# A retention layer with a swish MLP on one Trainium2 core: attention insertions merged, and loads, casts and transposes of the last batches moved

## The chip, the core and the metric

The kernel runs on one core of a Trainium2 chip. The metric is device microseconds of one execution. Times of the kernel before are 294.99 us in the median of three runs (294.67 to 295.45).

The engines are named as in the profile: PE is TensorE (matmuls; PEld its weight loads), DVE is VectorE, ACT is ScalarE, POOL is GpSimd, SP is SyncE. SPq stands for SP's queue of transfers: every load, store and DMA transpose here but one is issued by SP, in program order.

## The reference: what is computed

Eight batches (B = 8) of eight heads (H = 8), 576 rows (S) and a head size of 64 (D). Attention without softmax, with a decay per head:

```python
scores = scale * np.matmul(q, k.transpose(0, 1, 3, 2))
gamma = 1.0 - 2.0 ** (-5.0 - np.arange(H, dtype=np.float32))
Dmat = np.where(rel >= 0, gamma[:, None, None] ** rel[None, :, :], 0.0)
ret = scores * Dmat[None, :, :, :]
return np.matmul(ret, v).astype(np.float32)
```

Its result, as x of 4608 rows by 512, goes through an MLP: h = x @ w_in (512 to 2048), g = h * sigmoid(beta * h), out = g @ w_out (2048 to 512).

## The kernel before, in words

**Blocks of the MLP.** The rows are cut into nine blocks of 512: of each batch the first 512 rows (MB), and as block 8 the last 64 rows of all eight batches together, the tail. Blocks are worked in the order 0 to 6, 8, 7. A block is an up phase and a down phase. `up` (L717) makes one of 16 columns of the hidden layer: four matmuls of 512 columns into a PSUM bank `ph` (L724), then an activation on ACT into `gT` (L726). `down` (L750) makes a quarter of one of four row groups `ms`: four matmuls into the bank `po` (L759), and after the last quarter a copy to `ot` (L766) and a store.

**Attention in insertions.** The attention of batch u must be done before block u's up phase reads `xT`. It is cut in pieces that are inserted between the MLP's matmuls as runs of small 64x64 matmuls:
- `d_sc` (L478, matmuls L489): scores of eight chunks of 64 rows. Its first half (x = 0) uses the first pair of transposed keys `kT` of the batch, its second half (x = 1) the second pair; each half is 32 matmuls into two PSUM banks `sc`. `masks` (L496) multiplies them on DVE by a triangle into `R`.
- `d_st` (L500, matmuls L507): the products of keys and values of four chunks, 32 matmuls; its `chain` (L515, L519) adds them to running states on DVE and copies the states to `sbd` on ACT.
- `d_out` (L522): the products of `R` and values (L538, 64 matmuls), then of queries and states (`cross`, L551, 56 matmuls in two parts). The second part waits for a small DVE memset, the fence (L542). `evict` (L566) copies four banks `O` to `xT`, on DVE and ACT by turns.

`scores(u)` (L954) is one insertion: d_st(u, 1) and both halves of d_sc(u), in this order on PE. `outputs(u)` (L961) is d_out(u) with d_st(u + 1, 0). `early_states(2)` (L951) is d_st(2, 0) alone. The tail counts as u = 8.

**Data of a batch.** `load_q` (L84) brings q in two transfers of 512 KB, `load_kv` (L96) a quarter of k and one of v, 256 KB each. On POOL `pre_q` (L294) scales q, `pre` casts k (L323) and scales v (L301). `x_q` and `x_k` (L331) are DMA transposes of q and k, two each for a batch: x_k(b, 0) makes the first pair of `kT`, x_k(b, 1) the second. The program gives the transfers eight DMA semaphores in turn, so that each waits for the eighth before it.

**What sets the order.** The scheduler is off; the order of each engine is the order in which the code is recorded. `fill` is a list of 16 up steps and 16 down steps of a block; a step is four full matmuls. `base[n]` is the place of the n-th block's first step, written b4, b5, b6 for blocks 4 to 6. `streams` are lists of pairs (place in fill, step), and `merged` (L779) records all of them by place, each just ahead of the fill step of that number. `pair_prep` (L970) gives the places at which the data of a pair of chunks are loaded, cast and transposed, counted back from `at`. So a place decides what stands ahead of what on SP, POOL, DVE, ACT and PE alike.

PSUM has eight banks in four groups by tag: mm 3, O 2, sc 2, st 1. The `ph` and `po` of the MLP use mm.

Of the kernel before, what the change touches and what calls it, by code (L numbers as in the profile page):

```python
# [19 lines left out]
def kernel(  # L20
# [88 lines left out]
    tail_tiles, tail_q = {}, []  # L109
# [168 lines left out]

    def pre_q(b, n):

        if n == 0:
            batch[b] = dict(qs=sb.tile([P, CB, H, D], BF16, name="qs", tag="qs", bufs=2),
                            qT=sb.tile([P, CB, HP, P], BF16, name="qT", tag="qT", bufs=2))
# [12 lines left out]

    def pre(i, js=(0, 1)):

        b, c = seq[i]
        if 0 not in js:  # L300
            nc.gpsimd.tensor_tensor(live[i]["vn"], kv_tiles.pop(i)[:, 1], gains(gv, c), ALU.mult)  # L301
            return
        if c % 2 == 0:
            vns[b, c // 2] = sb.tile([P, 2, H, D], BF16, name="vn", tag="vn", bufs=VB)
        vn = vns[b, c // 2][:, c % 2]
        if b is None:
            tq, tk, tv = tail_tiles.pop(c)
            qk = sb.tile([P, 2, H, D], BF16, name="kn", tag="kn", bufs=4)
            qkT = sb.tile([P, 2, HP, P], BF16, name="kT", tag="kT", bufs=4)
            for to, hs in turned:  # L310
                nc.gpsimd.tensor_tensor(qk[:, 0, to], tq[:, hs], gains(gq, CB)[:, hs], ALU.mult)  # L311
                nc.gpsimd.tensor_copy(qk[:, 1, to], tk[:, hs])
            nc.gpsimd.tensor_tensor(vn, tv, gains(gv, CB), ALU.mult)
# [7 lines left out]
        live[i] = dict(kn=kn[:, c % 2], kT=kT[:, c % 2], vn=vn)  # L321
# [11 lines left out]
    def x_q(b, u):  # L333
        turn(batch[b]["qT"][:, 2 * u:2 * u + 2], batch[b]["qs"][:, 2 * u:2 * u + 2])
# [17 lines left out]
    def half(x):  # L352
        return slice(x * D, (x + 1) * D)
# [123 lines left out]

    def d_sc(u, xs=(0, 1)):  # L478

        R = {x: sb.tile([P, 2, 2, HP, TL], BF16, name="R", tag="R", bufs=4) for x in xs}  # L480
        sc = {}
        for x in xs:
            for j in range(2):
                sc[x, j] = psum.tile([P, 2, HP, TL], F32, name="sc", tag="O" if x and u > 1 else "sc", bufs=2)
            for cl in range(2):
                for p in range(HP):
                    for j, hh in spread:
                        c = 4 * x + 2 * cl + hh
                        nc.tensor.matmul(columns(u, sc[x, j][half(hh), cl, p, :]), piece(u, c)["kT"][half(j), p, half(hh)],  # L489
                                         q_of(u, c, j, p), start=cl == 0 and p == 0, stop=True, skip_group_check=True)  # L490
        mask = tri[1 if u == B else 0][:].unsqueeze(1).to_broadcast([P, 2 * HP, TL])
        batch.setdefault(u, {})["R"] = R

        def masks(x):
            for j in range(2):
                nc.vector.tensor_tensor(R[x][:, j].rearrange("k c p q -> k (c p) q"),  # L496
                                        sc[x, j].rearrange("k c p q -> k (c p) q"), mask, ALU.mult)
        return masks

    def d_st(u, x):  # L500

        S = [psum.tile([P, 2, HP, D], F32, name="st", tag=t, bufs=n) for t, n in (("st", 1), ("O", 2) if u == 1 else ("mm", 3))]
# [19 lines left out]
    def d_out(u):  # L522
# [10 lines left out]
        if u >= B - 1:  # L533
            own = [(cc, pp + 2 * y, hh, hh if other else 1 - hh)
                   for other in range(2) for cc in range(CB) for pp in range(2) for y in range(2) for hh in range(2)]
        for n, (cc, p, hh, j) in enumerate(own):
            h = head_of(u, p, j)
            last = nc.tensor.matmul(to(2 * cc + hh, p, h % 2), piece(u, 2 * cc)["vn"][half(hh), h, :],  # L538
                                    columns(u, R[cc // 2][half(hh), j, cc % 2, p, :]),
                                    start=cc == p % 2 == 0, stop=False, skip_group_check=True)  # L540
            if n + 1 == (len(own) if u < B - 1 else len(own) // 2):
                fence = nc.vector.memset(fenced[:], 0.0)  # L542
                after(fence, last)

        def cross(flip):
            for n, (cc, pp, y, j) in enumerate((cc, pp, y, j) for cc in range(CB) for pp in range(2) for y in range(2) for j in range(2)):
# [6 lines left out]
                if flip and n < 2:  # L553
                    after(m, fence)

        cross(0)

        def evict():
            for n, ((hh, y), o) in enumerate(O.items()):
# [6 lines left out]
                (nc.scalar.copy if n % 2 else nc.vector.tensor_copy)(x, o)  # L566
        return lambda: cross(1), evict
# [176 lines left out]
    pos_, ots, held = {}, {}, []  # L744

# [4 lines left out]
    def down(m, ms, f0, fn=4, n0=0, nn=d_model):  # L750

        gT = gts[m]
        if f0 == 0:
            pos_[ms] = psum.tile([P, d_model], F32, name="po", tag="mm" if m or ms < 3 else "st", bufs=3 if m or ms < 3 else 1)
# [11 lines left out]
        (nc.scalar.copy if m == 0 else nc.vector.tensor_copy)(ot, po[:, :nn])  # L766
# [184 lines left out]
    def early_states(u):  # L951
        d_st(u, 0)()

# [14 lines left out]
    lo6 = base[B - 2] + 3  # L968

    def pair_prep(i, at):  # L970
        b, c = seq[i]
        if b is None:
            early, late = ((-23, -12, -7), (-18.5, -8, -6.5)) if c == 0 else ((-11, -3, 7.5), (-6, 1, 8))
            return [(lo6 + x, f) for j, at3 in enumerate((early, late))
                    for x, f in zip(at3, (F(load_tail, c + j), F(pre, i + j), F(x_tail, i + j)))]
# [6 lines left out]
        if c == 0:  # L982
            if b == XB + 1:
                st += [(at - 30.1, F(load_kv, n)), (at - 30, F(x_k, XB, 1)), (at - 30, F(load_kv, n + 1))]
            sooner = 4 if b == B - 1 else 0
            st += [(at - 30 - sooner, F(load_q, b, (u,))) for u in range(2)] + [(at - 20 - sooner + x, F(pre_q, b, x)) for x in range(4)]
            st += [(at - (18 if b > B - 3 else 14) + 1.5 * x, F(x_q, b, x)) for x in range(2)]
        early = b == XB + 1 and c > 0
        loads = [] if b == XB + 1 and c == 0 else [(at - 29.7 + x / 10, F(load_kv, n + x)) for x in range(2)] if early else \
            [(at - 28 + 2 * x - (7 if b == B - 1 and c else 5 if b == B - 1 else 4 if b == B - 2 and c else 0), F(load_kv, n + x)) for x in range(2)]  # L990
        soon, turn_k = (24 if c else 20, 19 if c else 15.5) if b == B - 1 else (22, 11.5) if b == XB + 1 and c == 0 else (16, 13 if c else 11.5)
        return st + loads + [(at - soon, F(pre, i)), (at + 1 - soon, F(pre, i + 1)), (at - turn_k, F(x_k, b, c // 2))]

    streams.append([(base[1] + 17, F(early_states, XB))])
    for n in range(1, B - 1):
        lo, hi = (base[n] + 17, base[n + 1] - 9.5) if n == 1 else (base[n] + 3, base[n + 1] - 14)
        at = (lo, hi)
        work = [(n + 1, hi - 0.5, hi + 6)] if n == 1 else [(n + 1, hi - 1, hi + 6.5)]
        if n == B - 2:
            at = (lo, lo + 7, lo + 14, lo + 18)  # L1000
            work = [(B - 1, lo + 7, lo + 12.5), (B, lo + 20.5, lo + 25.5)]
        for x, t in enumerate(at):
            streams.append(pair_prep((n + 1) * CB + 2 * x, t))
        for u, t, t2 in work:
            streams.append([(t, F(scores, u)), (t2, F(outputs, u))])
# [31 lines left out]
```

## Time and profile before

| what | number |
|---|---|
| median of three runs | 294.99 us |
| the profiled execution's own time | 294.8 us |
| its span in the profile | 293.1 us |
| granted PE clock | 1.00 |
| busy: PE, PEld | 284.2 us, 147.0 us |
| busy: DVE, ACT, POOL | 104.2 us, 145.9 us, 109.9 us |
| bytes moved by DMA | 53.99 MB, mean 184 GB/s |
| median from issue to landing: q, k, v load | 5.9, 5.9, 5.3 us |
| the same: transpose of k, of q; store | 4.6, 3.6; 3.6 us |

A row of the groups or of the timeline names the line in the code, the engine, the operation, what is written and read, and how many there are. In a timeline the first column is the start from the beginning of the span and the second the length, both in us; a bracket at the end gives idle time of that engine just before, and what ended it. The chain of work that ended last is followed back from the last instruction, at each step to what released it. Records of a few matmuls are missing from the trace. Blocks 2 to 5 take about 30.2 us each: block 4's up phase starts at 141.8 us, its down phase at 155.5 us, block 5 at 172.2 us.

### The profile page before, as it was taken

The numbers are of one execution on the slowest core, as the hardware profiler recorded it, in microseconds if no ns is written. First come the engines' busy times: TensorE is split into PE (matmuls) and PEld (weight loads), VectorE is DVE, ScalarE is ACT, GpSimd is POOL, SyncE is SP. The second block draws the span as 40 slices with busy tenths as digits, with TensorE's granted clock in tenths as the row PEclk, the third lists the DMA queues.
The fourth block names the chain that finished last, engine by engine and source line by source line (L and its number), as shares of the span: only waits on it lengthen the run. The fifth ranks groups of instructions, "written<-read, shape, count | busy, mean of one in ns | idle before, by whom it ended". The sixth has DMA issues, their size and how long they took to land.

```text
span 293.1 us, 7933 instructions
## 1 busy us (share of the span) xinstructions
PE 284.2 (97%) x3373; PEld 147.0 (50%) x3404; DVE 104.2 (36%) x223; ACT 145.9 (50%) x262; POOL 109.9 (37%) x219
## 2 busy tenths in 40 slices
PE   7899999999999999999999999999999999999995
PEld 2554456885544554455445544554554544444443
DVE  5874566606620650065104520354053500110012
ACT  5566537882387335743473348334870168007600
POOL 3866037954640834371329407763422000000000
PEclk9999999999999999999999999999999999999999
DMA  7999999999999999949999939989896210131011
GB/s 222 304 366 386 378 279 266 188 179 242 231 139 268 282 192 242 235 74 163 234 241 210 197 105 273 187 177 228 200 176 106 73 39 0 36 72 38 0 72 72
DMA packets 121986, 53.99 MB, mean 184 GB/s; under 512 B 97744, under 2 KB 114400, under 8 KB 121952
## 3 DMA queue, kind: packets, MB, share of 16 engines
q1 hardware_dynamic: 121920, 53.49, 82.4%
q8 instruction: 26, 0.43, 0.7%
q14 instruction: 8, 0.07, 0.1%
q10 hardware_dynamic: 32, 0.01, 0.0%
HBM read 36.71 MB, written 9.44 MB: 157 GB/s over the span
## 4 chain that ended last, share of the span: by engine, by line
PE 94%; DMA 2%; issue 1%; POOL 1%; SPq 1%; DVE 0%; POOLq 0%
PE po L759 42%; PE ph L724 38%; PE ph L739 4%; DMA kvn<-in_k_dram 2%; PE sc L489 2%; PE O L538 2%; PE st L507 2%; PE O L551 1%; POOL kn L373 1%; PE st L448 1%; PE O L417 0%; SPq L104 0%; POOL vn L373 0%; PE ph L892 0%; SPq L84 0%
## 5 line engine op out<-in xcount | busy, mean ns | idle before, releaser
L759 PE MATMUL po<-w_out_sb,gT 128*128 128x512 bf16 (+2 forms) x573 | 125.1, 373 | 2.4 <-issue 2.1
L726 ACT ACTIVATE gT<-ph,beta_sb 128x512 bf16<-128x512 f32 (+1 forms) x144 | 91.3, 643 | 48.0 <-PE ph L724 47.6
L724 PE MATMUL ph<-xT,w_in_sb 128*128 128x512 bf16 (+1 forms) x567 | 113.3, 357 | 0.5
L759 PEld LDWEIGHTS <-gT 128*128 128x128 bf16 x593 | 56.1, 98 | 63.8
L724 PEld LDWEIGHTS <-w_in_sb 128*128 128x128 bf16 x576 | 56.0, 98 | 55.2 <-DVE first L515 0.5
L766 DVE COPY ot<-po 128x512 f32<-128x512 f32 (+2 forms) x33 | 22.2, 672 | 72.3 <-PE po L759 69.6
L496 DVE TENSOR_TENSOR R<-sc,tri 128x512 bf16<-128x512 f32 x30 | 18.7, 682 | 61.5 <-PE sc L489 61.5
L294 POOL TENSOR_TENSOR qs<-qn,gq 128x256 bf16<-128x256 f32 (+1 forms) x36 | 26.5, 764 | 37.3 <-DMA qn<-in_q_dram 36.0
L323 POOL CAST kn<-kvn 128x128 bf16<-128x128 f32 (+1 forms) x78 | 22.7, 331 | 30.7 <-DMA kvn<-in_k_dram 30.6
L301 POOL TENSOR_TENSOR vn<-kvn,gv 128x512 bf16<-128x512 f32 x26 | 27.1, 1045 | 4.9 <-DMA kvn<-in_v_dram 4.4
L566 ACT CAST xT<-O 128x512 bf16<-128x512 f32 x14 | 7.5, 589 | 31.8 <-PE O L551 31.8
L519 ACT CAST sbd<-warm 128x256 bf16<-128x256 f32 x18 | 7.3, 405 | 25.7 <-DVE warm L515 20.7
L739 PE MATMUL ph<-xT,w_in_sb 128*128 128x512 bf16 x54 | 12.5, 379 | 0.1
L515 DVE TENSOR_TENSOR warm<-st,first 128x256 f32<-128x256 f32 x20 | 8.4, 421 | 9.6 <-PE st L507 8.4
L515 DVE TENSOR_TENSOR first<-st,warm 128x256 f32<-128x256 f32 x25 | 10.6, 425 | 2.5
L566 DVE CAST xT<-O 128x512 bf16<-128x512 f32 x14 | 9.0, 686 | 5.7 <-PE O L551 5.7
L742 ACT ACTIVATE gT<-ph,beta_sb 128x512 bf16<-128x512 f32 x14 | 8.6, 687 | 4.5 <-PE ph L739 4.4
L311 POOL TENSOR_TENSOR kn<-tln,gq 128x128 bf16<-128x128 f32 (+1 forms) x12 | 5.7, 472 | 13.1 <-DMA tln<-in_q_dram 8.3
L212 POOL CAST w_in_sb<-wt 128x256 bf16<-128x256 f32 (+1 forms) x15 | 7.8, 538 | 4.7 <-DMA wt<-in_moe_w_in_dram 4.7
L519 ACT CAST sbd<-first 128x256 bf16<-128x256 f32 x18 | 7.3, 405 | 2.3 <-DVE first L515 0.3
L739 PEld LDWEIGHTS <-w_in_sb 128*128 128x128 bf16 x56 | 5.2, 98 | 6.1 <-issue 0.3
L229 DVE TENSOR_SCALAR w_out_sb<-wt,rbeta_sb 128x512 bf16<-128x512 f32 x13 | 5.9, 484 | 5.1 <-DMA wt<-in_moe_w_out_dram 5.1
(133 smaller groups left out, 164.6 us busy)
## 6 DMA issues: line engine op xcount, KB each, us to landing
qn<-in_q_dram SPq DMA_DIRECT2D x16, 512.0 KB, 5.9
kvn<-in_k_dram SPq DMA_DIRECT2D x32, 256.0 KB, 5.9
kvn<-in_v_dram SPq DMA_DIRECT2D x32, 256.0 KB, 5.3
out_dram<-ot SPq DMA_DIRECT2D x31, 256.0 KB, 3.6
wt<-in_moe_w_out_dram SPq DMA_DIRECT2D x8, 512.0 KB, 9.4
wt<-in_moe_w_in_dram SPq DMA_DIRECT2D x5, 512.0 KB, 9.5
wt<-in_moe_w_in_dram SPq DMA_DIRECT2D x6, 256.0 KB, 5.7
tln<-in_q_dram SPq DMA_DIRECT2D x8, 128.0 KB, 4.4
```

The source lines that it names most:

```text
L294: nc.gpsimd.tensor_tensor(batch[b]["qs"][:, cs, to], q_tiles[b][:, hs, cs].rearrange("p h i d -> p i h d"), gq[:, cs, hs].unsqueeze(3).to_ ...
L301: nc.gpsimd.tensor_tensor(live[i]["vn"], kv_tiles.pop(i)[:, 1], gains(gv, c), ALU.mult)
L323: nc.gpsimd.tensor_copy(kn[:, c % 2, to], t[:, 0, hs])
L496: nc.vector.tensor_tensor(R[x][:, j].rearrange("k c p q -> k (c p) q"), sc[x, j].rearrange("k c p q -> k (c p) q"), mask, ALU.mult)
L515: nc.vector.tensor_tensor(new[:], add, sums[(c - 1) % 2][:], ALU.add)
L519: e((sbq[c] if c < NC - 1 else ends[u])[:], new[:])
L566: (nc.scalar.copy if n % 2 else nc.vector.tensor_copy)(x, o)
L724: nc.tensor.matmul(ph, w_in_sb[:, ko, fo * P:(fo + 1) * P], xts[m][:, ko, :, w], start=(ko == 0), stop=(ko == KO - 1))
L726: nc.scalar.activation(gts[m][:, fo, :, w], ph, ACT.Silu, scale=beta_sb[:, fo:fo + 1])
L739: nc.tensor.matmul(phs[f][:], w_in_sb[:, ko, f * P:(f + 1) * P], xts[m][:, ko], start=(ko == 0), stop=(ko == KO - 1))
L759: nc.tensor.matmul(po[:, x:y], gT[:, fo, ms, :], w_out_sb[:, fo, n0 + x:n0 + y], start=(fo == 0), stop=(fo == FO - 1), skip_group_check=m < 2)
L766: (nc.scalar.copy if m == 0 else nc.vector.tensor_copy)(ot, po[:, :nn])
```

## The change

- Batch 2: early_states is gone; `scores_with_states(2, 2)` does its two state products between the two halves of its scores, two steps ahead of where scores(2) was (base[2] - 12 instead of base[2] - 10). The copy of the first row group's `po` of block 1 goes to ACT (`on_scalar`).
- Batches 3, 4 and 5: scores at the same places, outputs of 3 and 4 too.
- Batch 6: its scores are made together with the outputs of batch 5, in one insertion `outputs_with_scores(5, 6)` at b5 - 4 (outputs(5) was at b5 - 7.5, scores(6) at b6 - 15). Their banks are mm, mm and mm, st. The copy of block 4's third row group goes to ACT, and all four copies of the outputs to `xT` too.
- Batch 7: its scores are made together with both state products of batch 6, `scores_with_states(7, 6)`, at b5 + 16, the border of block 5's up and down phases. outputs(6) stays at about b6 - 8, and `last_scores` (second state product of batch 7, scores of the tail) is at b6 + 16, outputs(7) at b6 + 22, the tail's outputs at b6 + 28.5 as before.
- The data of batches 6 and 7 are placed by a new `whole_prep`, which for each batch first places loads of q and k and v, then casts of k, transposes, and scaling of v. The tail's loads, casts and transposes get new places too.
- Batch 2's second key transpose is recorded ahead of batch 3's first k load instead of behind it.
- The tail's scaled q and cast k use the tiles of the tag `qs` instead of `kn`; `qT` and `vn` tiles are taken later.

The core of the diff:

```diff
@@ -475,31 +484,35 @@
+    BANKS = dict(mm=3, O=2, sc=2, st=1)
+
+    def d_half(u, x, tags):
+
+        R = batch.setdefault(u, {}).setdefault("R", {})
+        R[x] = sb.tile([P, 2, 2, HP, TL], BF16, name="R", tag="R", bufs=4)
+        sc = [psum.tile([P, 2, HP, TL], F32, name="sc", tag=t, bufs=BANKS[t]) for t in tags]
...
-    def d_st(u, x):
+    def d_st(u, x, tags=None):
...
@@ -965,14 +982,32 @@
+    def scores_with_states(u, s):
+        first = d_half(u, 0, ("mm", "mm"))
+        first()
+        chains = [d_st(s, 0, ("O", "O")), d_st(s, 1, ("sc", "sc"))]
+        d_half(u, 1, ("mm", "st"))()
+        for f in chains:
+            f()
+
+    def outputs_with_scores(u, v):
+        first = d_half(v, 0, ("mm", "mm"))
+        first((0,))
+        cross, evict = d_out(u, plain=True)
+        first((1,))
+        second = d_half(v, 1, ("mm", "st"))
+        cross()
+        evict(es=(nc.scalar.copy,) * 2)
+        second()
+
+    def last_scores():
+        chain, masks = d_st(B - 1, 1), d_sc(B)
+        chain()
+        for x in range(2):
+            masks(x)
...
@@ -981,28 +1016,39 @@
-                st += [(at - 30.1, F(load_kv, n)), (at - 30, F(x_k, XB, 1)), (at - 30, F(load_kv, n + 1))]
...
+                st += [(at - 30.1, F(x_k, XB, 1)), (at - 30, F(load_kv, n)), (at - 30, F(load_kv, n + 1))]
...
+    def whole_prep(b, q_in, kv_in, q_pre, k_pre, q_turn, k_turn, v_pre):
+        i, st = b * CB, [(q_in + u / 2, F(load_q, b, (u,))) for u in range(2)] + [(q_pre + x, F(pre_q, b, x)) for x in (0, 2)]
+        st += [(q_turn + 1.5 * u, F(x_q, b, u)) for u in range(2)] + [(k_turn + 1.5 * u, F(x_k, b, u)) for u in range(2)]
+        for x in range(CB):
+            st += [(kv_in + x, F(load_kv, full.index(i + x))), (k_pre + x, F(pre, i + x, (0,))), (v_pre + x, F(pre, i + x, (1,)))]
+        return st
...
-    streams.append([(base[1] + 17, F(early_states, XB))])
-    for n in range(1, B - 1):
+    for n in range(1, B - 3):
...
+        if n == 1:
+            on_scalar.add((1, 0))
+            streams.append([(base[2] - 12, F(scores_with_states, XB, XB)), (hi + 6, F(outputs, XB))])
+        else:
+            streams.append([(hi - 1, F(scores, n + 1))] + ([(hi + 6.5, F(outputs, n + 1))] if n < B - 4 else []))
+    b4, b5, b6 = base[B - 4], base[B - 3], base[B - 2]
+    streams.append(whole_prep(B - 2, b4 - 2, b4, b4 + 6, b4 + 10, b4 + 12, b4 + 15.5, b4 + 14))
+    streams.append(whole_prep(B - 1, b4 + 18, b4 + 19, b4 + 20, b4 + 24, b5 - 3, b4 + 27, b5 - 3))
...
+    on_scalar.add((B - 4, 2))
+    streams.append([(b5 - 4, F(outputs_with_scores, B - 3, B - 2)), (b5 + 16, F(scores_with_states, B - 1, B - 2)),
+                    (b6 - 8, F(outputs, B - 2)), (b6 + 16, F(last_scores)), (b6 + 22, F(outputs, B - 1)), (b6 + 28.5, F(outputs, B))])
```

The pair of batch 5's last chunks is still placed by `pair_prep`: its k and v loads at b4 - 10 and b4 - 8, its casts at b4 + 2 and b4 + 3, and its transpose x_k(5, 1) at b4 + 5, as before. scores(5) is recorded at b4 + 17.

More of the change, by code (lines that the diff above doesn't have):

```diff
@@ L107 @@
     span_tiles = {}
-    tail_tiles, tail_q = {}, []
+    tail_tiles, tail_q, tail_qk = {}, [], {}
     def load_tail(t):
@@ L476, in after @@
         tc.add_manual_dep(later.ins, earlier.ins.name, mybir.DependencyInfo(mybir.DependencyClass.Sync, mybir.DependencyReason.DATA))
-    def d_sc(u, xs=(0, 1)):
[L480 to L498, printed above, removed]
@@ L500, in d_st, with masks @@
-    def d_st(u, x):
-        S = [psum.tile([P, 2, HP, D], F32, name="st", tag=t, bufs=n) for t, n in (("st", 1), ("O", 2) if u == 1 else ("mm", 3))]
+    BANKS = dict(mm=3, O=2, sc=2, st=1)
[3 more added lines that the diff above has]
+        sc = [psum.tile([P, 2, HP, TL], F32, name="sc", tag=t, bufs=BANKS[t]) for t in tags]
+        for cl in range(2):
+            for p in range(HP):
+                for j, hh in spread:
+                    c = 4 * x + 2 * cl + hh
+                    nc.tensor.matmul(columns(u, sc[j][half(hh), cl, p, :]), piece(u, c)["kT"][half(j), p, half(hh)],
+                                     q_of(u, c, j, p), start=cl == 0 and p == 0, stop=True, skip_group_check=True)
+        mask = tri[1 if u == B else 0][:].unsqueeze(1).to_broadcast([P, 2 * HP, TL])
+        def masks(js=(0, 1)):
+            for j in js:
+                nc.vector.tensor_tensor(R[x][:, j].rearrange("k c p q -> k (c p) q"),
+                                        sc[j].rearrange("k c p q -> k (c p) q"), mask, ALU.mult)
+        return masks
@@ L503, in d_st @@
+    def d_sc(u, xs=(0, 1)):
+        parts = {x: d_half(u, x, ("O", "O") if x and u > 1 else ("sc", "sc")) for x in xs}
+        return lambda x: parts[x]()
+    def d_st(u, x, tags=None):
+        S = [psum.tile([P, 2, HP, D], F32, name="st", tag=t, bufs=n) for t, n in [(t, BANKS[t]) for t in tags or ("st", "O" if u == 1 else "mm")]]
         for cl in range(2):
@@ L532, in d_out, with products, cross @@
         own = [(cc, p, hh, j) for cc in range(CB) for p in range(HP) for hh, j in spread]
-        if u >= B - 1:
+        if u >= B - 1 and not plain:
             own = [(cc, pp + 2 * y, hh, hh if other else 1 - hh)
                    for other in range(2) for cc in range(CB) for pp in range(2) for y in range(2) for hh in range(2)]
[L536 to L546, printed above, removed]
+        def products(own, at):
+            for n, (cc, p, hh, j) in enumerate(own):
+                h = head_of(u, p, j)
+                last = nc.tensor.matmul(to(2 * cc + hh, p, h % 2), piece(u, 2 * cc)["vn"][half(hh), h, :],
+                                        columns(u, R[cc // 2][half(hh), j, cc % 2, p, :]),
+                                        start=cc == p % 2 == 0, stop=False, skip_group_check=True)
+                if n + 1 == at:
+                    fence = nc.vector.memset(fenced[:], 0.0)
+                    after(fence, last)
+            return fence
+        def cross(flip, fence=None):
+            n = 0
+            for cc, pp, y, j in [(cc, pp, y, j) for cc in range(CB) for pp in range(2) for y in range(2) for j in range(2)]:
                 c, p = 2 * cc + (j ^ flip), pp + 2 * y
@@ L565, in evict @@
                     o = o.rearrange("k p i c s -> k (p i) c s")
-                (nc.scalar.copy if n % 2 else nc.vector.tensor_copy)(x, o)
-        return lambda: cross(1), evict
+                es[n % 2](x, o)
+        fence = products(own, len(own) if u < B - 1 or plain else len(own) // 2)
+        cross(0)
+        return lambda: cross(1, fence), evict
     def o_pre(j, a, e=nc.gpsimd):
@@ L744 @@
     pos_, ots, held = {}, {}, []
+    on_scalar = set()
     def release(n):
@@ L991, in pair_prep @@
-        soon, turn_k = (24 if c else 20, 19 if c else 15.5) if b == B - 1 else (22, 11.5) if b == XB + 1 and c == 0 else (16, 13 if c else 11.5)
+            [(at - 28 + 2 * x, F(load_kv, n + x)) for x in range(2)]
+        soon, turn_k = (22, 11.5) if b == XB + 1 and c == 0 else (16, 13 if c else 11.5)
         return st + loads + [(at - soon, F(pre, i)), (at + 1 - soon, F(pre, i + 1)), (at - turn_k, F(x_k, b, c // 2))]
-    streams.append([(base[1] + 17, F(early_states, XB))])
-    for n in range(1, B - 1):
-        lo, hi = (base[n] + 17, base[n + 1] - 9.5) if n == 1 else (base[n] + 3, base[n + 1] - 14)
[L997 to L1002, printed above, removed]
-            streams.append(pair_prep((n + 1) * CB + 2 * x, t))
-        for u, t, t2 in work:
-            streams.append([(t, F(scores, u)), (t2, F(outputs, u))])
+    def whole_prep(b, q_in, kv_in, q_pre, k_pre, q_turn, k_turn, v_pre):
[4 more added lines that the diff above has]
+        return st
```

49 lines of the change are left out of this document (26 added, 23 removed).

## The prediction

> **What bounds the kernel now.** I read the page's busy times first, then its chain of work that ended last, then that chain in order of time.
>
> ```profile
> PE 284.2 (97%) x3373; PEld 147.0 (50%) x3404; DVE 104.2 (36%) x223; ACT 145.9 (50%) x262; POOL 109.9 (37%) x219
> PE 94%; DMA 2%; issue 1%; POOL 1%; SPq 1%; DVE 0%; POOLq 0%
> ```
>
> TensorE (PE) is the bound; no other engine passes 50%. After 25 us PE runs full matmuls of 512 columns, one each 0.216 us, with **insertions** of small 64x64 attention matmuls between them. So the change can win only what insertions cost, and lose only where PE must wait. An insertion, from PE's timeline (start, length, line):
>
> ```profile
> 95.00 1.03 PE L759 MATMUL po<-w_out_sb,gT 128*128 128x512 bf16 x4
> 95.96 0.45 PE L507 MATMUL st<-vn,kn 64*64 64x64 bf16 x32
> 96.23 0.76 PE L489 MATMUL sc<-qT,kT 64*64 64x64 bf16 x64
> 97.14 6.85 PE L759 MATMUL po<-w_out_sb,gT 128*128 128x512 bf16 x31 [0.16 <-issue]
> ```
>
> The fourth full matmul starts at 95.00 + 3 x 0.216 = 95.65, the next recorded one at 97.14; less one slot of 0.216 that is 1.28 us. But 31 full matmuls are recorded up to the next insertion where the program has 32: the first record after the insertion is missing, so the insertion takes 1.28 - 0.22 = 1.06 us for 96 small matmuls. In the same way early_states at 65 us takes 0.47 us for 32 and outputs at 104 us 1.55 us for 152. The slopes are 0.59/64 = 9.2 ns and 0.49/56 = 8.7 ns a matmul, so about 0.2 us is **fixed per insertion**.
>
> The next view is SP's timeline around the start of block 4 (141.8 us), because SP issues every load, store and DMA transpose in program order.
>
> ```profile
> 142.00 1.68 SPq L772 DMA_DIRECT2D out_dram<-ot  x2
> 145.79 1.23 SPq L331 DMA_TRANSPOSE kT<-kn  x1
> 147.08 1.16 SPq L84 DMA_DIRECT2D qn<-in_q_dram  x2
> 148.28 0.51 SPq L96 DMA_DIRECT2D kvn<-in_k_dram  x1
> 148.83 2.32 SPq L96 DMA_DIRECT2D kvn<-in_v_dram  x1
> 151.20 2.57 SPq L96 DMA_DIRECT2D kvn<-in_k_dram  x1
> 153.81 1.00 SPq L96 DMA_DIRECT2D kvn<-in_v_dram  x1
> ```
>
> The transpose at 145.79 is x_k(5, 1), the second half of batch 5's keys. It waits for POOL's casts, is issued ahead of batch 6's loads, and lands at 149.0. Its reader is the second half of scores(5):
>
> ```profile
> 156.43 0.45 PE L507 MATMUL st<-vn,kn 64*64 64x64 bf16 x32
> 156.71 0.87 PE L489 MATMUL sc<-qT,kT 64*64 64x64 bf16 x64
> 157.73 0.38 PE L759 MATMUL po<-w_out_sb,gT 128*128 128x512 bf16 x1 [0.16 <-issue]
> ```
>
> The second 32 of the 64 sc begin 32 x 9 ns after 156.71, at 157.0. So the keys have 8 us to spare now.
>
> **The change, part by part.**
>
> 1. *Fewer insertions.* Small and full matmuls stay the same in number (1680 small ones from early_states on); insertions go from 15 to 13: early_states joins scores(2), scores(6) joins outputs(5), and scores(7) with states 6 takes the place of two. Two times 0.2 = **-0.4 us**. In the last blocks PE also waits 0.09 us for a ScalarE activation at 214.5 us, behind the state copies of scores(7) (matmul starts 306 ns apart instead of 216); that insertion moves to the border of the up and down phases, where no activation follows the copies: -0.1. Three gaps of 0.1 us inside insertions (157.0, 195.7, 218.1 us), with no wait at those instructions, may stay or go: 0 to -0.3, taken as -0.1. Sum **-0.6 us**.
>
> 2. *New readers and banks, covered.* Batch 2's insertion starts at 67.8 us instead of 70.0. Its second key half is now transposed right behind the first (issued 61.8, landed 66.2), so it lands about 67.5; it is read after sc 32 + st 64, at 67.8 + 96 x 9 ns = 68.7. Cover 1.2 us; without it PE waits the shortfall. The bank for that half is emptied by ScalarE (on_scalar, about 0.64 us from 67.9, done 68.6): 0 to 0.1 lost. The first down after it needs the first mask (VectorE 0.68 us from 68.3): 69.0 against 69.1. The eight state adds end near 75, outputs(2) starts at 77. At outputs(5) with scores(6) the fence sits behind one mask, which ends 1.3 us into the insertion, while cross(1) comes at 1.5. ScalarE's four xT evictions (0.59 each) take 2.4 us against 16 x 0.216 = 3.5 us of downs before their reader. At scores(7) the banks come free as activations 13 to 15 end, each within 0.1 us of need. All at 0, at most +0.3 together.
>
> 3. *Data sooner: what the keys of batch 5 meet.* In the new SP order whole_prep puts batch 6's two q loads (b4 - 2) and eight k and v loads (b4 to b4 + 3) **ahead of x_k(5, 1)** (b4 + 5), which keeps its place. Its keys are ready as before (145.8), but the program uses eight DMA semaphores in turn, so each transfer waits for the eighth before it, and transfers land in order: all 87 issued from 37 to 160 us landed in the order of issue. Landing by landing: batch 5's last v lands at 145.9 now, 145.7 then; store 0.6 (142.0 to 146.5 to 147.2: 0.65 apart); two q loads 1.65 + 1.6 (1.6 apart at 95, 123, 154 us; 2.8 once); store 0.6; eight k and v loads at 1.1 (0.92 to 1.2 where several follow each other, at times 2.2); the transpose 0.9 behind loads. That is 145.7 + 0.6 + 3.25 + 0.6 + 8.8 + 0.9 = **159.85**. SP issues it when the eighth before it, batch 6's first k, has landed (about 151.3), so issue is not what is last. PE wants it at 157.0 - 0.2 (part 1, batch 2's share) = 156.8. PE waits **3.0 us** in the middle of scores(5). The ends: all at their fastest (0.55, 3.1, 0.55, 8 x 0.92, 0.85) gives 158.1, a wait of 1.3; at their slowest (0.65, 4.5, 0.65, 8 x 1.2, 1.4) 162.5, a wait of 5.7. I take 3.0, from the rows met most often. Nothing can hide it: PE takes its matmuls in order, so all that stands behind these 32 waits too, and nobody's work becomes shorter.
>
> 4. *What follows.* The four transposes of batch 6 come directly behind and land by about 164; they are read at outputs(5), near 169.7 with the wait in. Batch 7's loads land to about 177, its transposes by about 183; scores(7) comes near 188.6. POOL's tail products wait for outputs(6) (near 197) and need some 11 us (per tail piece 3 products of 0.47, 3 casts of 0.35, 1.04); their last transpose lands near 212, last_scores is at 219. Cover of 5 us or more each: 0.
>
> **Sum**: -0.6 + 3.0 = +2.4 us on the profiled run's 294.8 us (span 293.1 and 1.7 around it), so 297.2. That run lies 0.2 under the median 294.99, so the forecast for a median is **297.3 us**.
>
> **Rivals.**
>
> *A, the forecast*: the key transpose is held behind batch 6's loads, PE waits 1.3 to 5.7 us. For it: the SP order is in the program, and no transfer overtook another. Chance 0.77.
>
> *B, the transpose does not stand behind the loads' data.* Mechanism: it is issued at about 151.3 and lands 3.2 to 4.6 us later, as the 145.79 one (3.2) and the 61.85 one (4.3) did, whatever is still in flight. It decides if it lands by 156.8. Then only part 1 is left: 294.8 - 0.6 + 0.2 = 294.4, not slower. Against it: the transpose at 87.9 us, with four stores ahead, took 4.9 us and landed last. Chance 0.13 (with a small remainder of a wait under 1.3 us).
> The Trainium skill, page "DMA: Bandwidth & Descriptors", section "Queues, rings and completion order", says that completion is not first in, first out for an issuing engine, since a DMA that uses fewer rings may finish earlier. The trace's 87 landings in order do not show that.
>
> *C, the wait also costs clock.* PE would idle longer than anywhere in this trace after its first matmul (0.35 us at most, at 9.9 us), and the granted clock is 1.00 throughout, so no row shows what an idle PE loses. Bounds: nothing, or half speed for as long as it stood idle, 3.0 us of work done at half rate, +1.5: 298.8. Chance 0.06.
> The Trainium skill, page "TensorE: Matmul & The Clock Gate", section "Why this matters for your kernels", wants no gap over about 3 us, one idle window setting the clock to half. By its window of 3.4 us C would add an estimated 1.7 us; a free-running window is not surely filled by 3 us.
>
> *D, a second late arrival* (batch 6's keys at outputs(5), batch 7's at scores(7)): needs transfers 5 us slower than worked out; 1 to 3 us more, 299.3. Chance 0.04. That the change does not do what it says is part of A: data comes sooner for batch 6 and later for batch 5.
>
> **Chances.** Over 0.3% (0.9 us, about what a measurement of this kernel can tell) slower: A but for waits under 1.5 us, C, D: 0.82. Within: most of B and those short waits: 0.14. Faster: B with all small gains: 0.04. Range 295.6 to 299.6 leaves out B and the worst of A, C and D.
>
> **What would show it.** Right: in scores(5) PE's sc group (32 + 32) is split by an idle time of about 3 us that a DMA kT ends, near 157 to 160 us; SP's line shows the kT transpose after eight kvn loads; every other insertion reads 0.2 us + 9 ns a matmul; later blocks are shifted by a constant. Wrong: no idle time there (B), granted clock under 1.00 after it (C), or PE waiting at outputs(5) or scores(7) (D).

## The result: slower, with one long wait and a lowered clock

| what | before | changed |
|---|---|---|
| median | 295.22 us (six runs, 294.67 to 295.57) | 299.5 us (six runs, 297.97 to 300.58) |
| ratio | | 1.0143, 95% interval 1.0121 to 1.0165 |
| the profiled execution: time, span | 294.8 us, 293.1 us | 300.51 us, 298.8 us |

The change makes the kernel 4.3 us slower in the median; the sum of the prediction was +2.4 us, 297.3 us for a median. First the changed kernel's page: busy times, the shares of the chain that ended last, and the group of the scores' matmuls.

```profile
PE 285.8 (96%) x3375; PEld 147.5 (49%) x3404; DVE 101.5 (34%) x219; ACT 148.4 (50%) x266; POOL 109.2 (37%) x219
...
PE 87%; SPq 5%; DMA 4%; issue 1%; POOL 1%; DVE 0%; POOLq 0%
...
L498 PE MATMUL sc<-qT,kT 64*64 64x64 bf16 x416 | 5.7, 195 | 3.9 <-DMA kT<-kn 3.9
```

PE's share of the chain falls from 94% to 87%, and SP's queue and DMA have 9% where they had 3%: for a stretch the end hangs on transfers. The scores' row names the transfer, the key transpose. PE's timeline of the changed kernel shows the place, the second half of scores(5):

```profile
156.70 0.45 PE L520 MATMUL st<-vn,kn 64*64 64x64 bf16 x32
156.98 0.44 PE L498 MATMUL sc<-qT,kT 64*64 64x64 bf16 x32
161.26 0.45 PE L498 MATMUL sc<-qT,kT 64*64 64x64 bf16 x32 [3.85 <-DMA kT<-kn]
161.90 1.91 PE L779 MATMUL po<-w_out_sb,gT 128*128 128x512 bf16 x4 [0.19 <-issue]
```

The 64 scores that stood together before are split by 3.85 us of idle time. And the four full matmuls behind them take 1.91 us, where four took 1.03 before. The table by stretches of the changed kernel says why; its columns are the stretch, its length, the busy time and number of instructions of five engines, the granted clock, the DMA share and GB/s.

```profile
155.00:157.00 2.00, 2.00 (x45) 0.89 (x46) 0.00 (x0) 1.37 (x2) 0.88 (x3) 1.00 0.96 214
157.00:161.00 4.00, 0.41 (x52) 0.30 (x37) 1.29 (x2) 0.00 (x0) 2.56 (x7) 1.00 1.18 222
161.00:163.00 2.00, 1.55 (x35) 0.90 (x37) 1.23 (x3) 0.00 (x0) 2.00 (x3) 0.71 1.06 202
163.00:165.00 2.00, 2.00 (x6) 0.72 (x5) 1.66 (x5) 1.22 (x3) 1.20 (x2) 0.50 1.10 71
165.00:167.00 2.00, 2.00 (x10) 0.82 (x9) 0.69 (x1) 0.41 (x1) 0.00 (x0) 0.94 1.14 227
```

Behind the wait the clock is 0.50; the trace's clock record has it so for 3.41 us from 161.83 us. Single matmuls start 0.427 us apart there instead of 0.216, so about 1.7 us more are lost. From scores(5) to outputs(5) the changed kernel takes 16.23 us (last full matmul ahead of each at 156.39 and 172.62), and 10.57 us in e8 below, which has neither wait nor low clock: 5.66 us, 4.0 from the wait and 1.7 from the clock. That is nearly the whole 6.1 us by which its span is longer than e8's (292.7 us). Against the kernel before the spans differ by 5.7 us. PE waits for data nowhere else after 25 us.

Five of the six runs show a clock under 0.995; the one at 1.00 is the fastest, 297.97 us. The profiled execution is one of the two slowest, 1.0 us over the median, so its sums are not those of the median.

### The profile page after: what moved, and what is told of

It reads as the page before. It is cut to its first block, busy times and chain, and to the rows that moved or that the text cites. A ratio compares the mean times of both kernels' runs of the same rounds, so it can differ in the third digit from the quotient of the medians.

```text
span 298.8 us, 7946 instructions
## 1 busy us (share of the span) xinstructions
PE 285.8 (96%) x3375; PEld 147.5 (49%) x3404; DVE 101.5 (34%) x219; ACT 148.4 (50%) x266; POOL 109.2 (37%) x219
## 4 chain that ended last, share of the span: by engine, by line
PE 87%; SPq 5%; DMA 4%; issue 1%; POOL 1%; DVE 0%; POOLq 0%
PE po L779 42%; PE ph L742 33%; PE ph L757 4%; SPq L96 4%; DMA kvn<-in_k_dram 2%; PE sc L498 2%; PE O L552 1%; DMA kT<-kn 1%; PE st L520 1%; PE O L567 1%; POOL kn L382 1%; SPq L84 1%; PE st L457 1%; PE O L426 0%; SPq L104 0%
## 5 line engine op out<-in xcount | busy, mean ns | idle before, releaser
L779 PE MATMUL po<-w_out_sb,gT 128*128 128x512 bf16 (+2 forms) x574 | 127.0, 376 | 2.1 <-issue 1.6
L786 DVE COPY ot<-po 128x512 f32<-128x512 f32 (+2 forms) x31 | 20.8, 671 | 72.5 <-PE po L779 68.5
L581 ACT CAST xT<-O 128x512 bf16<-128x512 f32 x16 | 8.5, 591 | 25.9 <-PE O L567 25.9
L498 PE MATMUL sc<-qT,kT 64*64 64x64 bf16 x416 | 5.7, 195 | 3.9 <-DMA kT<-kn 3.9
L786 ACT COPY ot<-po 128x512 f32<-128x512 f32 x6 | 3.5, 586 | 11.8 <-PE po L779 11.8
L581 DVE CAST xT<-O 128x512 bf16<-128x512 f32 x12 | 7.7, 686 | 4.3 <-PE O L567 4.3
```

Source lines behind the costliest of these rows:

```text
L581: es[n % 2](x, o)
L779: nc.tensor.matmul(po[:, x:y], gT[:, fo, ms, :], w_out_sb[:, fo, n0 + x:n0 + y], start=(fo == 0), stop=(fo == FO - 1), skip_group_check=m < 2)
L786: (nc.scalar.copy if m == 0 or (m, ms) in on_scalar else nc.vector.tensor_copy)(ot, po[:, :nn])
```

## The experiments

Ratios are to the kernel before, with 95% intervals; the table gives also the wait for data that PE has in each profiled execution.

| run | median us | ratio | wait for data, scores(5) / batch 7's scores |
|---|---|---|---|
| changed kernel | 299.5 | 1.0143 [1.0121, 1.0165] | 3.85 / 0 |
| e4_loads_alone | 301.24 | 1.0210 [1.0191, 1.0229] | 4.44 / 0 |
| e2_kept_busy | 300.70 | 1.0194 [1.0181, 1.0207] | 1.24 / 0 |
| e6_busy_f32 | 298.82 | 1.0136 [1.0101, 1.0171] | 1.49 / 0 |
| e3_six_ahead | 297.03 | 1.0071 [1.0049, 1.0093] | 1.41 / 0.28 |
| e1_keys_first | 296.90 | 1.0071 [1.0047, 1.0095] | 0 / 2.61 |
| e5_hold_block4 | 296.42 | 1.0055 [1.0030, 1.0080] | 0 / 2.24 |
| e7_more_instructions | 298.51 | 1.0115 [1.0095, 1.0135] | 0 / 0 |
| e8_hold_block3 | 294.42 | 0.9979 [0.9967, 0.9991] | 0 / 0 |
| e9_ready_stores | 294.43 | 0.9974 [0.9963, 0.9985] | 0 / 0 |
| e10_before_held | 296.40 | 1.0041 [1.0017, 1.0065] | 0 / 0; tail 0.45 |
| e11_before_held_late | 294.89 | 1.0000 [0.9985, 1.0014] | 0 / 0 |
| e12_after_held_late | 294.69 | 0.9992 [0.9982, 1.0001] | 0 / 0 |

### Is it the order on SP?

The theory at first was the prediction's: the key transpose is late because ten loads stand ahead of it. **e4_loads_alone** puts this one part of the change into the kernel before.

```diff
-            st += [(at - 30 - sooner, F(load_q, b, (u,))) for u in range(2)] + ...
+            st += [((b4 - 2 + u / 2) if b == B - 2 else at - 30 - sooner, F(load_q, b, (u,))) for u in range(2)] + ...
...
+        if b == B - 2:
+            loads = [(b4 + c + x, F(load_kv, n + x)) for x in range(2)]
```

> The kernel before with one part of the change alone: batch 6's two q loads at b4 - 2 and its eight k and v loads at b4 to b4 + 3, so ahead of x_k(5, 1), and every insertion, cast and other transfer where it was. Theory (these ten loads alone are the loss, the rest of the change is worth -0.35): PE waits for the keys in scores(5) about 4 us, its clock falls after it for about 1.7 us more, and the time is 299.5 to 301, that is at least as slow as the changed kernel. Rival (the loss needs the merged insertions or the other moved steps, through their banks or readers): under 297 us.

301.24 us, just over what was expected, a wait of 4.44 us at the same place, and clocks of 0.988 to 0.994 in all four runs. In the profiled execution the low clock lasts 6.83 us, twice as long as in the changed kernel. So the ten loads, moved in the kernel before, are enough for the whole loss, without the merged insertions. The next two take them away in doses: **e3_six_ahead** leaves six of the eight k and v loads ahead, **e1_keys_first** none.

```diff
-    streams.append(whole_prep(B - 2, b4 - 2, b4, b4 + 6, ...
+    streams.append(whole_prep(B - 2, b4 - 2, b4 + 2.5, b4 + 6, ...   (e3)
+    streams.append(whole_prep(B - 2, b4 - 2, b4 + 5.1, b4 + 6, ...   (e1)
```

> The changed kernel with batch 6's k and v loads at b4 + 2.5 instead of b4: six of the eight loads stay ahead of x_k(5, 1) on SP, the last two go behind it. Theory (a load ahead costs the keys one landing, 1.24 us each in the trace of the changed kernel, 9.94 us for eight): the keys land 2.5 us sooner, at about 158.7, the wait is 1.4 us instead of 3.85 and too short for the clock to fall, so 299.5 - 2.5 - 1.7 = 295.3 to 296.3 us. Rival (one late transfer or SP's own stall makes the wait, not the number of loads): the keys land at 161 as before, or at 150 as with none ahead, so 299.5 or 294.7 us.

> The changed kernel with one place altered: batch 6's eight k and v loads stand at b4 + 5.1 instead of b4, so x_k(5, 1) is issued ahead of them and only the two q loads stay ahead of it. Theory (order on SP's queue): the key transpose is issued near 147 us and lands near 150, PE reads its keys at 157 without a wait, the clock stays at 1.00, and what is left of the change is the merged insertions, measured at -0.35 us in the trace of the changed kernel: 294.3 to 295.0 us. Batch 6's keys come about 2 us later than in the changed kernel and are still in time for outputs(5). Rival (the early loads as such slow everything that moves then, whatever the order): the wait stays at 1 us or more, or turns up at outputs(5) in front of batch 6's keys: 296 us or more.

In e3 the wait is 1.41 us, as worked out, with the clock at 1.00 in all four runs. The profiled execution, 296.04 us, is in the expected range; the median, 297.03 us, is 0.7 us over it, and a wait of 0.28 us that nobody expected stands in front of batch 7's scores. In e1 the first wait is gone. But e1 takes 296.9 us where 294.3 to 295.0 were expected. The time is the rival's, but the place of the new wait was named by neither theory. PE's timeline of e1:

```profile
184.69 1.24 PE L742 MATMUL ph<-xT,w_in_sb 128*128 128x512 bf16 x5
188.53 0.45 PE L498 MATMUL sc<-qT,kT 64*64 64x64 bf16 x32 [2.61 <-DMA qT<-qs]
```

PE wants batch 7's turned q near 185.9 us, and it lands near 188.4. In the changed kernel the same transposes are no sooner; PE simply comes to them at 192 us, since it has lost 5.7 us before. **The first wait hid a second one**, so taking the first away gives back only part of it.

### Why is batch 7 late too?

The theory formed on this was that until about 188 us transfers run one behind another without a pause, so that each one taken away counts. **e5_hold_block4** is e1 with block 4's stores issued later.

```diff
-            if m < 2:
+            if m < 2 or m == 4:
                 held.append((rows[:, ms, n0:n0 + nn], ot))
...
+    streams.append([(b6 + 8, F(release, 4))])
```

> The kernel of e1_keys_first with block 4's four stores held back and issued late in block 6 (b6 + 8), behind everything that the scores of batch 7 need. In e1 PE waited 2.6 us for batch 7's second q transpose at scores_with_states(7, 6), at 185.9 us. Theory (one cause for both waits: until about 188 us the transfers run one behind the other without a pause, and the change asks for batch 7's data before they can all be through; each transfer taken out of the way brings that data about 0.65 us sooner): three of the four stores stood ahead of those transposes, so they land about 2 us sooner, the wait falls from 2.6 to 0.6 us or less, the clock does not fall, and the time is e1's 296.9 - 2.0 - 0.5, near 294.5. Rival (the q transposes are late because they stand behind the key transpose on SP, which waits for casts on POOL; stores do not matter): the wait stays at 2.6 us and the time at 296.9.

296.42 us; the wait falls only from 2.61 to 2.24 us, so this theory failed. **e8_hold_block3** is the changed kernel, all ten loads ahead of the keys, with block 3's stores held instead (m == 3, released at b5 + 20).

> The changed kernel with block 3's four stores held back to b5 + 20, all transfers of batch 6 still ahead of x_k(5, 1). Theory (what counts is how many transfers stand ahead, of whatever kind): two of the four stores stood among the loads ahead of x_k(5, 1) and two shortly before; the keys land 1.6 to 3 us sooner, the wait of 3.85 us falls to 0.9 to 2.2 us, the clock holds; batch 7's q transposes land near 188 still, so the time is no lower than 295.5: 295.5 to 297.0. Rival (only loads ahead count, or SP's own stall): the wait stays within 0.5 us of 3.85 and the time at 299 or more.

294.42 us: no wait at either place, though only four transfers of 256 KB were moved. This is less than the 295.5 us that the theory allowed at the least, and the rival expected 299, so both failed. The reason is in SP's timeline of the changed kernel, ahead of the part that the prediction looked at:

```profile
122.43 0.98 SPq L96 DMA_DIRECT2D kvn<-in_v_dram  x1
132.28 0.36 SPq L792 DMA_DIRECT2D out_dram<-ot  x1
132.75 1.28 SPq L338 DMA_TRANSPOSE qT<-qs  x1
...
143.24 1.04 SPq L84 DMA_DIRECT2D qn<-in_q_dram  x2
144.38 0.45 SPq L792 DMA_DIRECT2D out_dram<-ot  x1
144.87 0.43 SPq L96 DMA_DIRECT2D kvn<-in_k_dram  x1
```

From 123.4 to 132.3 us SP issues nothing. The waits of SP between 115 and 160 us in the changed kernel (waited for: us in all, times, longest) name the cause:

```profile
SPq L792 <- DVE ot L786: 10.0, 2, 8.8
```

The first store of block 3 stands at the head of SP's queue and waits 8.8 us for DVE's copy of a row group, which ends at 132.25 us: the row group's last matmul comes at about 130.2 us (12 of its 16 follow the insertion that ends at 127.65), and state additions stand ahead of the copy on DVE. Batch 5's transposes and batch 6's loads, which need nothing from it, stand behind. The kernel before stands still at the same place, for 8.0 us:

```profile
122.92 1.02 SPq L96 DMA_DIRECT2D kvn<-in_v_dram  x1
132.01 0.36 SPq L772 DMA_DIRECT2D out_dram<-ot  x1
```

The same stretch in e8:

```profile
122.63 1.04 SPq L96 DMA_DIRECT2D kvn<-in_v_dram  x1
124.15 1.90 SPq L338 DMA_TRANSPOSE qT<-qs  x1
...
147.66 3.36 SPq L338 DMA_TRANSPOSE kT<-kn  x1
```

x_k(5, 1), at 147.66, is issued 9.3 us sooner than in the changed kernel (156.93), behind the same ten loads. **e9_ready_stores** tells the store's wait from its bytes: as many stores at the same places, but always those of the block before, whose copies are done.

```diff
-            if m < 2:
+            if m < 5:
                 held.append((rows[:, ms, n0:n0 + nn], ot))
+                if m in (3, 4):
+                    release(1)
...
+    streams.append([(b5 + 20, F(release, 4))])
```

> The changed kernel with the stores of blocks 2, 3 and 4 shifted: at each place where block 3 or 4 had a store, SP now issues the store of the block before, whose copy is long done; block 4's four stores go at b5 + 20. So from block 3 on as many transfers stand ahead of batch 5's and batch 6's data as in the changed kernel, but SP never stands still for a copy of DVE. Theory, formed after e8_hold_block3 (SP stood still from 123.4 to 132.3 us in front of block 3's first store, which waited for a copy on DVE, and everything behind it on SP was late by that): SP issues batch 5's transposes and batch 6's loads some 5 to 9 us sooner; no wait in scores(5), no wait at scores_with_states(7, 6), and the time is that of e8, 294.3 to 294.8 us. Rival (the number of transfers ahead, the theory of e1, e3 and e5, in which only e8's missing four stores helped): 296.5 us or more.

294.43 us and no wait. SP's timeline of e9 has no such pause in front of batch 5's first q transpose, and x_k(5, 1) is issued at 148.66 us:

```profile
122.11 0.85 SPq L767 DMA_DIRECT2D out_dram<-ot  x1
123.07 1.37 SPq L338 DMA_TRANSPOSE qT<-qs  x1
...
148.66 2.93 SPq L338 DMA_TRANSPOSE kT<-kn  x1
```

So it was the wait at the head of SP's queue, not the number of transfers. It takes two things together: the kernel before has the pause of SP but the old order, and PE waits for no data; e8 and e9 have the new order without the pause, and PE waits for none either; the changed kernel and e4 have both. e8 and e9 are faster than both kernels, by 0.2 to 0.3% against the kernel before.

### What do the merged insertions give by themselves?

**e10_before_held** and **e11_before_held_late** hold block 3's stores in the kernel before, **e12_after_held_late** is e8 with the release of e11 (base[6] + 22, instead of base[5] + 20 in e10).

> The kernel before with block 3's four stores held back to b5 + 20, as in e8_hold_block3, and nothing else. Theory (what e8 gains over the kernel before comes from the merged insertions, and holding stores back only takes a loss away that the change had made): PE waits for no data in the kernel before, so within 0.2 us of it, 294.7 to 295.1. Rival (the stores themselves cost the kernel before something, and e8's gain is theirs): 294.4, as e8.

e10 missed both expectations: 296.4 us. Its release puts four stores ahead of the tail's last two key transposes, which are issued at 221.93 us instead of 217.31, and PE waits there, as its timeline shows:

```profile
226.71 0.58 PE L489 MATMUL sc<-kT 64*64 64x64 bf16 x48
227.73 0.32 PE L489 MATMUL sc<-kT 64*64 64x64 bf16 x16 [0.45 <-DMA kT<-kn]
```

This and a pause of 0.58 us in outputs(2) that no engine ends make most of the 1.6 us in the one profiled execution:

```profile
78.63 0.22 PE L538 MATMUL O<-R,vn 64*64 64x64 bf16 x3 [0.58 <-issue]
```

This pause lies ahead of the first store that e10 moves, so it isn't of the edit's making. What the other executions lose is open; two of the twelve show a clock of 0.994.

> e10_before_held once more, with block 3's four stores released at b6 + 22 instead of b5 + 20. In e10 they went in front of the tail's last two key transposes, which SP issued at 221.9 us instead of 217.3, and PE waited 0.45 us for them; so e10 does not say what the stores themselves are worth. Theory (PE waits for no data in the kernel before, so holding stores back gives it nothing): no wait for data, 294.7 to 295.1 us. Rival (the stores cost the kernel before something, and the gain of e8 and e9 is theirs): 294.4.

> The changed kernel with block 3's four stores released at b6 + 22, that is e8_hold_block3 with the release of e11_before_held_late, for a pair that differs in the change alone. Theory (the merged insertions are worth about 0.5 us, as the sum over the insertions in the trace of e8 says, once no data are late): 294.3 to 294.6 us, 0.4 to 0.7 under e11. Rival (the gain came with the early release or with the stores): within 0.2 us of e11.

e11 stands at 294.89 us: the stores are worth nothing to the kernel before. e12 at 294.69 is 0.2 us under it, less than expected, and at the edge of what the rival allowed; its interval against the kernel before reaches 1.0001. Summed over the insertions after 60 us (what each takes beyond the full matmuls around it) and the activation wait near 214.5 us, e11 has 18.28 us and e12 18.01; the kernel before has 18.24 and e8 17.67. So the merging is worth 0.3 to 0.6 us in these profiled executions; the times of e11 and e12, the pair that differs in the change alone, don't set it apart from nothing. Most of the spread is one insertion, outputs(6): 1.57 us in e8 and e9, 1.84 to 1.88 in e11 and e12. Why is open.

### Is the lowered clock a loss of its own?

**e2_kept_busy** fills the idle time in the changed kernel with 14 full matmuls, **e6_busy_f32** with two float32 matmuls of 432 columns (recorded as four; they took 1.62 us, not the 3 us expected).

```diff
+        for _ in range(idle):
+            nc.tensor.matmul(sc[0].rearrange("k c p q -> k (c p) q"), ident[:], ident[:, :TL].unsqueeze(1).to_broadcast([P, 2 * HP, TL]),
+                             start=True, stop=True, skip_group_check=True)
```

> The changed kernel with 14 more full matmuls of 512 columns (identity, nothing of the result comes of them: the real scores start the same bank afresh) right ahead of the second half of scores(5), 14 x 0.216 = 3.02 us of work in the place of PE's idle time. The wait for the keys ends where it did (161.2 us), but PE idles for about 1 us of it instead of 3.85. Theory (part of the loss is a clock lowered after a long idle time): no slice with a granted clock under 1.00, the eight matmuls behind scores(5) stand 0.216 us apart, and the time is 1.7 us under that of the changed kernel, about 297.8. Rival (the low clock of the changed kernel has nothing to do with PE's idling): the clock falls again near 162 us and the time stays at 299.5.

> e2_kept_busy again with far fewer instructions: two float32 matmuls of 432 columns (about 3 us; nothing of the result comes of them) fill PE's idle time in scores(5) in place of 14 bf16 ones. In e2 the clock stayed at 1.00 but PE stood still 0.75 us at 176.3 and 0.93 us at 202.5, where nothing was late. Theory (those two pauses are PE's own instructions arriving late: 28 more of them moved the 256-instruction fetches against the big insertions): with 8 more instructions at most the pauses are gone, the clock stays at 1.00, and the time is 297.7 to 298.2. Rival (PE pays for being kept busy in some other way): the pauses are there again, 300.5.

In e2 all four runs keep a clock of 0.999 or 1.00, and the full matmuls after scores(5) start 0.216 us apart. So the low clock did come from PE's idling. The time did not fall with it, to 297.8 us, but stayed at 300.7. What the clock gave back (1.7 us), two pauses took again, which PE's timeline of e2 shows:

```profile
161.18 0.45 PE L501 MATMUL sc<-qT,kT 64*64 64x64 bf16 x32 [1.24 <-DMA kT<-kn]
...
177.08 0.38 PE L782 MATMUL po<-w_out_sb,gT 128*128 128x512 bf16 x1 [0.75 <-issue]
...
203.43 5.99 PE L782 MATMUL po<-w_out_sb,gT 128*128 128x512 bf16 x27 [0.93 <-issue]
```

"issue" means that nothing in the profile ended them. In e6, with few more instructions, they are gone, and its runs fall in two groups: 297.63 and 297.89 us at a clock of 0.999 and 0.998, 299.76 and 299.88 at 0.994 and 0.993. The two groups lie 2.1 us apart, near the 1.7 us that the low clock costs. The filling did not keep the clock each time: PE still idles 1.49 us behind it, and whether float32 matmuls with 16 output rows count as full work is open. Against the changed kernel the faster group can't be read as a pure effect of the clock, since the keys landed 1.0 us sooner in e6.

### The pauses

**e7_more_instructions** puts 14 tiny matmuls (0.13 us) at the same place into e5.

```diff
+        for _ in range(idle):
+            nc.tensor.matmul(sc[0][:, 0, 0], ident[:], ident[:, :TL], start=True, stop=True, skip_group_check=True)
```

> e5_hold_block4 with 14 more matmuls of 64 columns (0.13 us of work, 28 instructions; nothing of the result comes of them) at the place where e2_kept_busy had its 14 wide ones. Theory (PE's instructions are fetched 256 at a time, and after an insertion of 150 to 184 small matmuls the fetch is only just in time): a pause of 0.5 us or more that no other engine ends, some 3 us behind outputs_with_scores(5, 6) or outputs(6), with the fetch landing 1.4 us before its end, so 0.7 to 3 us over e5. Rival (the pauses of e2 had another cause): within 0.3 us of e5.

298.51 us, 2.1 over e5. PE's timeline of e7, behind outputs_with_scores(5, 6):

```profile
170.74 1.67 PE L781 MATMUL po<-w_out_sb,gT 128*128 128x512 bf16 x7
174.26 0.38 PE L781 MATMUL po<-w_out_sb,gT 128*128 128x512 bf16 x1 [1.85 <-issue]
```

The trace's DMA records hold a queue of the kind "instruction" with packets of 16,384 bytes: 26 in the changed kernel, 27 in e2. One runs from 171.40 to 172.71 us, and PE goes on 1.55 us after its end. The second pause, behind outputs(6) (matmul starts 1.97 us apart), ends 1.44 us after such a packet; the two of e2 end 1.4 us after theirs. The pause of e10 in outputs(2) ends 1.57 us after one, too (77.06 us). So PE stood still for its own instructions, as e7's expectation had it before the run; the 16 DMA engines were 90% busy or more while the packet of 171.40 us was under way. The two pauses also brought PE to batch 7's scores late enough for the wait there to vanish.

## Why the prediction came out as it did

- **The sum.** The forecast of 297.3 us was 2.2 us short. The step that failed is that the wait stands in the sum without the clock that it costs: rival C got a chance of 0.06 and no term, and the runs show 1.7 us. The second error is the size of the wait: 4.0 us instead of 3.0. The time lies just inside the range, 295.6 to 299.6 us, since the range was drawn wide enough for C and D, not since the sum was near. In the profiled execution, 3.3 us over the 297.2 worked out for it, the other 0.6 us are smaller: its start takes 0.3 us longer up to 47 us, and the insertions gave back about 0.3 of the 0.6.
- **Fewer insertions, -0.6.** Right in direction, at most right in size: -0.57 between e8 and the kernel before, -0.27 between e12 and e11, in times -0.2 to -0.7.
- **New readers and banks, at most +0.3.** Right: outputs(2) takes 1.57 us in e8 for 1.54 in e11, and scores_with_states(7, 6) 1.50 for the 1.35 of its twin of batch 2.
- **Data sooner, 3.0 us.** The mechanism, its place and the order of landing were right: a DMA kT ends the idle time in the middle of scores(5), and batch 6's transfers landed in the order of issue. The size was short by 1.0 us. The mis-sized term is "eight k and v loads at 1.1": they landed in 9.95 us, 1.24 each, not 8.8. The store ahead of them took 0.98 us for 0.6, the q loads 0.1 less than worked out, and so the keys landed at 161.22 instead of 159.85 us; PE came for them 0.5 us later than worked out. In e8 eight loads landed in 9.8 us as well, so 1.1 was too little for such a run of loads; why is open. The step "SP issues it when the eighth before it ... has landed (about 151.3), so issue is not what is last" was wrong, too. That load had landed at 151.39, but SP was still issuing the loads ahead, the last seven of them at 0.9 to 3.2 us each: ten loads and a store took it 13.7 us, and it issued the transpose at 156.93. Whether this made the keys later is open, since they landed 0.84 us behind the last load, as the sum had it (0.9).
- **Rival C, the clock, at 0.06.** The largest error. Its price, 1.5 us, was near the 1.7 measured; its chance was not: it came in five of six runs. The range given to the wait, 1.3 to 5.7 us, reached nearly twice as far as the 3.0 us on which C was priced, so C should have had a term in the sum. The Trainium skill, page "TensorE: Matmul & The Clock Gate", section "HAM oscillation — how this bites in real kernels", wants no idle gap over about 3.4 us; by it the 3.85 us here lose clock and the 3.0 us of the forecast do not. The trace agrees for 3.85 us, but e1's profiled execution lost the clock after a wait of 2.61.
- **What follows, cover of 5 us or more.** This failed unseen. Batch 7's transposes were put "by about 183", and they landed near 188.4 in e1, with PE there at 185.9. In the changed kernel the first wait covered it, so the measured time does not show the error. Rival D was thus not an addition to A but what stands behind it.
- **Rival B** fell: the key transpose landed behind all ten loads. Of the 87 transfers that the prediction counts as landed in order, the trace gives a landing for 66, and these are in order.
- What the working did not look at is SP's pause from 123 to 132 us, which is in the kernel before too. There it costs nothing (e11); the change brought forward the need for the data behind them, by 25 us for batch 7's scores (210.8 to 185.8 in e8).

## What to carry to other kernels

Before loads are moved sooner on a queue that issues in program order, look for what that queue waits on: a store that waits for its copy holds up all loads and transposes behind it, and issuing the store of the block before in its place cost nothing here (e9). After a wait is removed, look for the next reader that the wait had covered (e1). Price a wait of PE of two to four microseconds with the clock that it may cost, 1.7 us here.

## What the runs showed of the hardware

- After a wait of PE the granted clock fell to 0.50, for 3.41 us in the changed kernel and in e1, for 6.83 us in e4. These runs show no sharp limit of idle time. A clock under 0.995 is found in four of four runs with an idle time of 4.44 us in the profiled execution (e4), in five of six with 3.85 (changed kernel), three of ten with 2.61 (e1), four of twelve with 2.24 (e5), two of four in e6, with 1.49 us behind the float32 matmuls, and none of eight with 1.41 and 1.24 (e3, e2). It is also found in two of twelve runs of e10, whose profiled execution has no pause over 0.58 us, and in one of the 82 runs of the kernel before that were made beside the experiments. Other executions may have waited longer than the profiled one.
- Instructions of PE come in packets of 16,384 bytes. 26 packets for the 6808 matmuls and weight loads of e8 make about 260 instructions each, an estimate that leaves out PE's other instructions. An insertion of 184 matmuls with as many weight loads, 368 instructions in 1.85 us, uses more than one such packet. 28 instructions more in front of it were enough for pauses of 1.85 and about 1.75 us (e7). The Trainium skill, page "Runtime: NRT & Kernel Launch", section "Instruction fetch mechanics", gives blocks of 256 instructions and calls the crossing from one to the next mostly hidden; the size agrees, and e7 shows where it is not hidden.
